# Moving a third of GpSimd's scaling, two sums and six masks to other places in a fused linear-attention and feed-forward kernel

## The chip, the core and the metric

The kernel runs on one core of a Trainium2 chip. The metric is device time in microseconds (us) of one execution. A core has five engines that each work off their own instructions in order and wait for each other through semaphores: TensorE (PE in the profile; its weight loads are the row PEld), VectorE (DVE), ScalarE (ACT), GpSimd (POOL) and SyncE (SP), which here only issues DMAs. TensorE writes to PSUM, which VectorE and ScalarE read; the kernel lets GpSimd work on SBUF alone.

## The reference

Two stages. The first is attention with a decaying state: for each of 4 batches and 8 heads, over blocks of a sequence of 768 with head size 64,

```python
intra = np.einsum('bhic,bhjc->bhij', qb, kb) * Dmask[None]      # lam ** (i - j), lower triangle
intra = np.einsum('bhij,bhjd->bhid', intra, vb)
inter = np.einsum('bhid,bhde->bhie', qb * lam_pow[None], kv_state)
out[:, :, sl] = intra + inter
kv_state = lam_block * kv_state + np.einsum('bhsd,bhse->bhde', kb * rev_pow, vb)
```

The second stage takes this output as x, 3072 tokens by 512, and computes `((x @ w_a) * (x @ w_b)) @ w_out` with 1536 inner features. Inputs and output are float32.

## The kernel before

**Units and groups.** A unit is 128 tokens of one batch with all its heads; there are 24, numbered 0 to 23, six to a batch. The feed-forward part takes them in seven groups of 4, 2, 4, 4, 4, 4 and 2 units (`GROUPS`, L28), numbered 0 to 6. While a group's feed-forward part runs on TensorE, the attention of the next group's units is worked in between, piece by piece.

**Pieces of a unit's attention.** "P" (`prep_k`, L301) scales k and then q by powers of lam into bfloat16, two GpSimd instructions (L276), lets SP issue a DMA transpose of the result (L310) and loads of q and k of a later unit (`pump`, L194), and lets GpSimd issue the load of v (L298). "S" (`piece_S`, L446) multiplies keys with queries, eight matmuls of 64 rows into two PSUM banks kq (L343), and lets VectorE mask both banks (`mask`, L360), the one right behind the other. "V", "O2" and "Q" bring the state forward and compute the unit's output; "Q" has the scores of one more unit in it. The last output piece of a group lets VectorE build four sums of x, `xs` (L542 to L545), that the next group's feed-forward part needs.

**The feed-forward part of groups 1 to 6** (`ffn_seven`, L550) computes 2-by-2 block products with seven multiplications in place of eight. Its *first step* forms the products with w_a and w_b in six blocks of features, i = 0 to 5 (the two-unit groups, whose tiles are cut otherwise, are not touched by the change). Each block has seven products m1 to m7 of four matmuls 128x256 (groups of four units). They run over steps s: block i does m1 at s = 7i, m5 at 7i+2, m2 at 7i+3, m6 at 7i+4, m3 at 7i+6, m7 at 7i+8 and m4 at 7i+12; the last m4 runs inside the second step. What the others do for a block:

- m1 into bank q; ScalarE copies it (s1). m5 into bank r; ScalarE copies it (s5). m6 is added into q; ScalarE copies that (u2). m3 is added into r; m7 and m4 are added into q.
- c11 = s1 + m2. Either VectorE adds it straight from PSUM (L598), or ScalarE copies m2 (s2, the rows `s<-m_p`) and GpSimd adds the two (L601). `SUM_ON_VEC` (L42) lists the blocks that go the first way.
- c12 = u2 + r on VectorE (L609, two buffers); GpSimd multiplies ab = c11 * c12 (L611).
- c22 = s5 + q on VectorE after m7 (L615); after m4 VectorE multiplies ab = c22 * q (L618). m4 is added into the bank that c22 reads, so it waits for c22.

The *second step* of groups 2 to 5 (`out_seven`, L657) multiplies ab with w_out in the same manner; its first product o_q reads the ab of blocks 0, 2 and 4.

**What sets the order.** Everything is written out by hand: each engine runs its instructions in the order of the program. `hook(slot)` calls, between the products, the pieces that `PLAN[g]` lists for that slot. In the first step, an even slot 2n comes behind step s = 7n+1 and an odd slot 2n+1 behind s = 7n+4: slot 1 behind s = 4, slot 2 behind 8, slot 4 behind 15, slot 5 behind 18, slot 6 behind 22, slot 7 behind 25, slot 8 behind 29. Slots 12 and more are in the second step; slots 17, 18 and 19 follow each other, with only the last product o_q<-two,ab and a store behind them. "G" at slot 17 is a GpSimd copy of one element of `xs` (L1008): GpSimd's later work waits for the sums. PSUM has seven banks for all this; `ps_bank` (L123) takes the one that was used longest ago among those that are not held.

In the kernel before, group 3 scales units 17, 18 and 19 in its first step and 20 at slot 17; group 4 scales 21, 22 and 23 in its first step. Units 15, 18+19 and 22+23 get their "S" at slot 7 of group 3, at slots 18 and 19 of group 3, and at slots 18 and 19 of group 4.

Of the kernel before, what the change touches and what calls it, by code (L numbers as in the profile page):

```python
# [17 lines left out]
BF16 = mybir.dt.bfloat16  # L18
# [4 lines left out]
def _bc(ap, dims):  # L23
    import dataclasses
    return dataclasses.replace(ap, ap=dims)
# [13 lines left out]


S_GROUPS = (1, 2, 3, 4, 5, 6)
SUM_ON_VEC = {1: (2,), 2: (0, 1, 2, 3, 5), 3: (1, 2, 3, 4, 5), 4: (1, 2, 3, 4, 5), 5: (1, 2, 4, 5), 6: (0, 1, 2)}  # L42
O_SEVEN = (2, 3, 4, 5)
O_EARLY = (5,)
ACT_COPY = (4, 10, 12, 13, 14, 16, 17, 18, 20, 21)
# [17 lines left out]
}  # L63
for _g, _u in ((2, 10), (3, 14), (4, 18)):
    PLAN[_g] += [(11, "V", _u), (13, "Q", (_u, _u + 1, _u + 2)), (14, "V", _u + 2), (14, "S", _u + 3),
                 (16, "O2", (_u + 2, _u + 3)), (18, "S", _u + 4)] + ([(19, "S", _u + 5)] if _g > 2 else [])
PLAN[2] += [(_s, "W", None) for _s in (3, 3, 3, 4, 4, 4)]


# [1 line left out]
def kernel(  # L71
# [11 lines left out]
    nc = tc.nc  # L83
    B, H, S, D = q.shape
    BLK = 128
    NB = S // BLK
    HP = H // 2
# [13 lines left out]
    msk_pool = ctx.enter_context(tc.tile_pool(name="msk", bufs=4))  # L101
# [11 lines left out]
    bank = {"held": set(), "age": [0] * 7, "clock": 0}  # L113

    def touch(i):
        bank["clock"] += 1
        bank["age"][i] = bank["clock"]
# [5 lines left out]
    def ps_bank(name, shape, dt, hold=False, at=None):  # L123
        i = at
        if i is None:
            i = min((i for i in range(7) if i not in bank["held"]), key=lambda i: bank["age"][i])
        touch(i)
        if hold:
            bank["held"].add(i)
        bank["last"] = i  # L130
        return ps_pool.tile(shape, dt, name=name, tag=f"ps{i}")

    def read(i):
        if i is not None:
            touch(i)
# [54 lines left out]
    def wait_for(t):  # L190
        landed = singles.tile([1, 1], t.dtype, name="landed")
        nc.sync.dma_start(out=landed, in_=t[0:1, 0, 0:1])
# [68 lines left out]
    lotri_bc = _bc(lotri, [lotri.ap[0], [0, HP], lotri.ap[1]])  # L261
# [7 lines left out]
    U = {}  # L269
# [17 lines left out]
    def make_ks(u, eng):  # L287
        scale(eng, qk_of(u)[:, 1], raw.pop((u, "k")), lp_k[:, u % NB])

    def make_qs(u, eng):  # L290
        scale(eng, qk_of(u)[:, 0], raw.pop((u, "q")), lp_q[:, u % NB])
# [3 lines left out]
    def make_vb(u):  # L295
        b, nb = divmod(u, NB)
        vb = prep_pool.tile([128, H, D], BF16, name="vb", tag="vb", bufs=7)
        nc.gpsimd.dma_start(out=vb, in_=vr[b, nb])  # L298
        vbs[u] = vb

    def prep_k(u):  # L301
        make_ks(u, "dve" if u < n0 + 4 else "pool")
        make_qs(u, "pool")
        scaled(u)

    def scaled(u):
        used["u"] = u + 1
        if u in DMA_T:
            qkT = qkT_pool.tile([128, 2, HP, 128], BF16, name="qkT", tag="qkT")
            nc.sync.dma_start_transpose(  # L310
                out=qkT[:].rearrange("p j hp i -> p (j hp) i"),
                in_=U[u]["qk"][:].rearrange("p j h d -> p (j h d)"))
            U[u]["qT"], U[u]["kT"] = qkT[:, 0], qkT[:, 1]
        pump()

    def piece_T(u):
        d = U[u]
        tps = ps_bank("tps", [128, 2, HP, 128], BF16)
        for j in range(2):
            for hp in range(HP):  # L320
                nc.tensor.transpose(tps[:, j, hp, :], d["qk"][:, j, 2 * hp:2 * hp + 2, :], ident)
        qkT = qkT_pool.tile([128, 2, HP, 128], BF16, name="qkT", tag="qkT")
        nc.scalar.copy(qkT, tps)
        d["qT"], d["kT"] = qkT[:, 0], qkT[:, 1]
# [4 lines left out]
    def score_banks():  # L329
        kq = Banks()  # L330
        kq.ids = []
        for i in range(2):
            kq.append(ps_bank(f"kq{i}", [128, HP, 128], F32))
            kq.ids.append(bank["last"])
        return kq

    def scores(u, kq=None):
        d = U[u]
        kq = kq or score_banks()
        for hp in range(HP):  # L340
            for i in range(2):
                p = slice(64 * i, 64 * i + 64)
                nc.tensor.matmul(kq[i][:, hp, :], lhsT=d["kT"][p, hp, :], rhs=d["qT"][p, hp, :],  # L343
                                 start=True, stop=True, skip_group_check=True)
        return kq

    def masks(u, kq):
        ms = mask(kq)
        U[u]["m"] = lambda i, hp: ms[i][:, hp, :]

    def mask(kq, split=False):
        ms = []
        for i in range(2):
            m = msk_pool.tile([128, HP, 128], BF16, name=f"m{i}", tag=f"m{i}")
            if split and i == 1:
                raw_kq = a_pool.tile([128, HP, 128], BF16, name="raw_kq", tag="a")
                nc.scalar.copy(raw_kq, kq[i])
                nc.gpsimd.tensor_mul(m, raw_kq, lotri_bc)
            else:
                nc.vector.tensor_mul(m, kq[i], lotri_bc)  # L360
            read(getattr(kq, "ids", (None, None))[i])
            ms.append(m)
        return ms
# [81 lines left out]

    def piece_S(u):  # L446
        masks(u, scores(u))

    def piece_V(u):
        kv_update(u)  # L450
        if u % NB < NB - 1:
            kv_copy(u, kv["ps"], "act" if u in ACT_COPY else "dve")
# [97 lines left out]
    def ffn_seven(g, u0, n, xT, hook, last):  # L550
# [31 lines left out]
        def step(i, n):  # L582
# [10 lines left out]
            elif n == 2:  # L593
                p, pb = bank_of("m_p")
                product(i, p, w_of(wa_sb, 2, i), x12, True)
                d["c11"] = a_pool.tile([128, nf, h], BF16, name="c11", tag="a")
                if i in SUM_ON_VEC[g]:
                    nc.vector.tensor_add(d["c11"], d["s12"][:, 0], p)  # L598
# [184 lines left out]
    def store_kept():  # L783
        row, o_sb = kept.pop(0)
        nc.sync.dma_start(out=out_r[row], in_=o_sb)
# [62 lines left out]
    def new_xT(g):  # L848
        gx[g] = xT_pool.tile([128, KS, 512], BF16, name="xT", tag="xT")
        for i in range(GROUPS[g]):  # L850
            xTs[g_u0[g] + i] = (gx[g], i * BLK)
# [62 lines left out]
    for u in range(n0):  # L914
        U[u] = dict(kn=kn4[:, u], qT=xT4["q"][:, :, u * BLK:(u + 1) * BLK],
                    m=lambda i, hp, u=u: ms4[hp // 2, u // 2][i][:, 2 * (u % 2) + hp % 2, :])
# [61 lines left out]
    for g, n in enumerate(GROUPS):  # L978
        if g + 1 < len(GROUPS):
            new_xT(g + 1)  # L980
        plan = {}
        for slot, name, us in PLAN.get(g, ()):
            plan.setdefault(slot, []).append((name, us))

        def hook(slot, plan=plan):
            for name, us in plan.get(slot, ()):
                if name == "P":
                    prep_k(us)
                    if us in DMA_T:
                        make_vb(us)  # L990
                elif name == "QS":
                    make_qs(us, "pool")
                elif name == "KS":
                    make_ks(us, "dve")
                    scaled(us)
                elif name == "LS":
                    wait_for(raw[us - 2, "k"])
                    load_x("q", us, nc.sync)
                    load_x("k", us, nc.sync)
                elif name == "L":  # L1000
                    load_all(us)
                elif name == "TW":
                    w_sums(us)
                elif name == "TO":
                    wo_sums(us)
                elif name == "G":
                    gate = singles.tile([1, 1], BF16, name="gate")
                    nc.gpsimd.tensor_copy(gate, xs[max(xs)][0:1, 3, 0, 0:1])  # L1008
                elif name == "GT":
                    gate = singles.tile([1, 1], BF16, name="gate")  # L1010
                    nc.gpsimd.tensor_copy(gate, two[max(two)][0:1, 3, 0, 0:1])
                elif name == "W":
                    store_kept()
                elif name == "T":
                    piece_T(us)
                elif name == "S":
                    piece_S(us)
                elif name == "V":
                    piece_V(us)
                elif name == "O":  # L1020
                    pieces_O((us,))
                elif name == "O2":
                    pieces_O(us)
                else:
                    pieces_O(us[:2], us[2:])

        if g in S_GROUPS:
            ffn_seven(g, g_u0[g], n, gx.pop(g), hook, g + 1 == len(GROUPS))
        else:
            ffn(g_u0[g], n, gx.pop(g), hook, g == 0)  # L1030
# [29 lines left out]
```

## Time and profile before

| | us |
|---|---|
| Median of 4 runs (218.99 to 219.17) | 219.06 |
| The profiled execution, its own time | 218.99 |
| Its span, first to last instruction | 216.9 |
| PE, PEld, DVE busy in the span | 209.6, 162.7, 175.3 |
| ACT, POOL busy in the span | 109.1, 126.6 |
| First matmul of the first step of groups 2, 3, 4, 5 | 72.63, 105.03, 138.09, 169.94 |

TensorE is busy for 97% of the span, at a granted clock of 0.998. Busy does not mean at its best: a matmul's row has the time that it spends in the pipeline (273 ns for 128x256), while in a steady stream one starts every 109 ns, a product of four every 0.437 us. Losses are therefore read from the distance between the starts of two products, and from the chain of waits.

### The profile page before, as it was taken

The page shows a single profiled execution, that of the slowest core. Times are in us where ns is not written, and L with a number is a line of the kernel's source. Part 1 is how long each engine was busy: PE and PEld are TensorE (multiplying, and loading weights), DVE is VectorE, ACT ScalarE, POOL GpSimd, SP SyncE. Part 2 cuts the span into 40 slices and gives each one's busy share as a digit, 9 for nine tenths or more (in the row PEclk, how much of TensorE's full clock was granted, in tenths as well). Part 3 has the DMA queues.
Part 4 walks back from the last instruction along what each step waited for, and adds up shares of the span by engine and source line. Part 5 has one row for each costly group of instructions (what it writes and reads, how often), then busy time and mean ns, then how long its engine had stood idle before and what let it go on. Part 6 is the DMA issues. An engine that isn't in the chain of part 4 may idle for free.

```text
span 216.9 us, 5801 instructions
## 1 busy us (share of the span) xinstructions
PE 209.6 (97%) x2339; PEld 162.7 (75%) x2347; DVE 175.3 (81%) x320; ACT 109.1 (50%) x199; POOL 126.6 (58%) x144
## 2 busy tenths in 40 slices
PE   7799999999999999999999999999999999999993
PEld 2376444555996788878888887888987888889973
DVE  0892999878788987999588999788999787996860
ACT  2686224256872556436555535465535557343521
POOL 5879659973697199810999920699810246400320
PEclk9999999999999999999999999999999999999999
DMA  4999999999799989992699994499900500002202
GB/s 125 302 180 193 202 231 213 229 219 176 122 196 158 158 96 265 156 276 40 130 201 251 175 217 75 128 233 115 111 3 3 193 3 0 3 0 90 108 3 97
DMA packets 84654, 30.78 MB, mean 142 GB/s; under 512 B 71956, under 2 KB 81044, under 8 KB 84628
## 3 DMA queue, kind: packets, MB, share of 16 engines
q1 hardware_dynamic: 51636, 19.86, 45.7%
q0 software_dynamic: 32704, 10.49, 42.2%
q8 instruction: 18, 0.29, 0.6%
q10 hardware_dynamic: 288, 0.07, 0.1%
q14 instruction: 8, 0.07, 0.1%
HBM read 28.32 MB, written 6.29 MB: 160 GB/s over the span
## 4 chain that ended last, share of the span: by engine, by line
PE 84%; POOL 7%; DMA 3%; SPq 1%; ACT 1%; DVE 1%; issue 1%
PE m_q L564 20%; PE m_r L564 10%; PE op L801 10%; PE o_q L675 9%; PE o_r L675 5%; PE o_ps L379 5%; PE m_p L564 5%; PE b_ps L487 5%; PE a_ps L487 5%; PE kq L343 3%; POOL qk L276 3%; DMA k<-in_k_dram 3%; POOL ab L611 3%; PE o_p L675 2%; PE kvd L410 1%; SPq L229 1%
## 5 line engine op out<-in xcount | busy, mean ns | idle before, releaser
L564 PEld LDWEIGHTS <-tw 128*128 128x128 bf16 x576 | 48.9, 98 | 5.8 <-issue 0.3
L611 POOL TENSOR_TENSOR ab<-c,c 128x512 bf16<-128x512 bf16 x30 | 34.8, 1168 | 28.5 <-DVE c L609 28.2
L564 PE MATMUL m_q<-xs,tw 128*128 128x256 bf16 (+1 forms) x288 | 36.1, 255 | 0.0
L360 DVE TENSOR_TENSOR m<-kq,lotri 128x512 bf16<-128x512 f32 x47 | 29.5, 682 | 1.5 <-PE kq L343 1.5
L564 PEld LDWEIGHTS <-wa_sb 128*128 128x128 bf16 x288 | 24.7, 98 | 2.6
L579 ACT COPY s<-m_q 128x512 f32<-128x512 f32 x30 | 17.7, 590 | 17.1 <-PE m_q L564 15.5
L618 DVE TENSOR_TENSOR ab<-c,m_q 128x512 bf16<-128x512 f32 x30 | 20.6, 686 | 6.7 <-PE m_q L564 4.5
L609 DVE TENSOR_TENSOR c<-u,m_r 128x512 f32<-128x512 f32 x30 | 20.5, 682 | 5.9 <-ACT u L579 5.3
L298 POOL DMA_DIRECT2D vb<-in_v_dram x24 | 22.4, 933 | 1.5 <-DMA wo_sb<-in_moe_w_out_dram 1.2
L801 PE MATMUL op<-wo_sb,ab 128*128 128x512 bf16 (+2 forms) x114 | 22.1, 335 | 0.4 <-issue 0.2
L579 ACT COPY s<-m_r 128x512 f32<-128x512 f32 x30 | 17.7, 590 | 7.2 <-PE m_r L564 7.2
L579 ACT COPY u<-m_q 128x512 f32<-128x512 f32 x30 | 17.8, 595 | 6.3 <-PE m_q L564 6.0
L615 DVE TENSOR_TENSOR c<-s,m_q 128x512 f32<-128x512 f32 x30 | 20.6, 685 | 0.5
L675 PEld LDWEIGHTS <-sm 128*128 128x128 bf16 x192 | 17.5, 98 | 3.6 <-DVE sm L714 0.4
L598 DVE TENSOR_TENSOR c<-s,m_p 128x512 bf16<-128x512 f32 x23 | 15.8, 687 | 4.7 <-PE m_p L564 4.5
L276 POOL TENSOR_TENSOR qk<-qf,lp_q 128x512 bf16<-128x512 f32 x18 | 18.8, 1044 | 1.2 <-DMA qf<-in_q_dram 1.2
L601 POOL TENSOR_TENSOR c<-s 128x512 bf16<-128x512 f32 x7 | 9.1, 1293 | 16.4 <-ACT s L579 16.4
L402 ACT CAST xT<-o_ps 128x512 bf16<-128x512 f32 x22 | 11.9, 589 | 12.7 <-PE o_ps L379 12.4
L564 PE MATMUL m_q<-xT,tw 128*128 128x256 bf16 (+1 forms) x144 | 18.1, 255 | 0.1
L564 PE MATMUL m_r<-xs,tw 128*128 128x256 bf16 (+1 forms) x144 | 18.1, 255 | 0.0
L564 PE MATMUL m_q<-xT,wa_sb 128*128 128x256 bf16 (+1 forms) x144 | 18.1, 255 | 0.0
L564 PE MATMUL m_r<-xs,wb_sb 128*128 128x256 bf16 (+1 forms) x144 | 18.1, 255 | 0.0
(119 smaller groups left out, 375.6 us busy)
## 6 DMA issues: line engine op xcount, KB each, us to landing
out_dram<-o_two SPq DMA_DIRECT2D x8, 512.0 KB, 3.6
qf<-in_q_dram SPq DMA_DIRECT2D x14, 256.0 KB, 5.0
kf<-in_k_dram SPq DMA_DIRECT2D x14, 256.0 KB, 5.6
vb<-in_v_dram POOLq DMA_DIRECT2D x24, 128.0 KB, 5.5
wa_sb<-in_moe_w_a_dram POOLq DMA_DIRECT2D x6, 256.0 KB, 6.2
wb_sb<-in_moe_w_b_dram POOLq DMA_DIRECT2D x6, 256.0 KB, 7.6
wo_sb<-in_moe_w_out_dram POOLq DMA_DIRECT2D x6, 256.0 KB, 8.1
out_dram<-o_kept SPq DMA_DIRECT2D x6, 256.0 KB, 4.5
```

Of the source, the lines that this page charges most:

```text
L276: eng_of(eng).tensor_mul(dst.rearrange("p (c b) d -> p b c d", b=2), x[:].rearrange("p (b c) d -> p b c d", b=2), lp.rearrange("p (b c) o ...
L298: nc.gpsimd.dma_start(out=vb, in_=vr[b, nb])
L360: nc.vector.tensor_mul(m, kq[i], lotri_bc)
L487: nc.tensor.matmul(ps[:, lo:hi], lhsT=w_sb[:, s, f * 128:(f + 1) * 128], rhs=xT[:, s, lo:hi], start=(s == 0), stop=(s == KS - 1), skip_gro ...
L564: nc.tensor.matmul(ps[:, f, :], lhsT=w(k, f), rhs=x[:, k, :], start=(first and f == 0 and k == 0), stop=True, skip_group_check=True)
L579: nc.scalar.copy(t, ps)
L609: nc.vector.tensor_add(c12, d["u2"], d["r"])
L611: nc.gpsimd.tensor_mul(ab[:, nf * i:nf * i + nf, 0:h], d["c11"], c12)
L615: nc.vector.tensor_add(d["c22"], d["s5"], d["q"])
L618: nc.vector.tensor_mul(ab[:, nf * i:nf * i + nf, h:2 * h], d["c22"], d["q"])
L675: nc.tensor.matmul(ps[:, t, :], lhsT=x(j, c)[:, t * BLK:(t + 1) * BLK], rhs=w(j)[:, c, :], start=(first and t == 0 and j == js[0] and c == ...
L801: nc.tensor.matmul(op[:, lo:hi], lhsT=ab[:, f, t * 128:(t + 1) * 128], rhs=wo_sb[:, f, lo:hi], start=(f == 0), stop=(f == FC - 1))
```

## The change

Three things change, in groups 3, 4 and 5 alone. The order of all instructions up to 105 us in the profile stays.

- **Scaling.** Units 17 and 18, and 21 and 22, stay in the first step (slots 2 and 5 in place of 1 and 4). Units 19 and 23 move from slot 7 of the first step to slot 17, behind the gate on the sums of x, unit 19 ahead of unit 20.
- **Sums.** In groups 3 and 4 the c11 of block 0 is added by VectorE too; ScalarE's copy s2 and GpSimd's add of that block go.
- **Masks.** Unit 15 gets its scores at slot 6 of group 3 in place of slot 7; units 19 and 23 move from slot 19 of groups 3 and 4 to slot 6 of groups 4 and 5. The scores and the mask of the first bank come at slot 6, the mask of the second bank at slot 8; that bank is held in between.

```diff
-SUM_ON_VEC = {..., 3: (1, 2, 3, 4, 5), 4: (1, 2, 3, 4, 5), 5: (1, 2, 4, 5), 6: (0, 1, 2)}
+SUM_ON_VEC = {..., 3: range(6), 4: range(6), 5: (1, 2, 4, 5), 6: (0, 1, 2)}
...
-    3: [(1, "P", 17), (4, "P", 18), (7, "S", 15), (7, "P", 19), (17, "G", None), (17, "P", 20)],
-    4: [(1, "P", 21), (4, "P", 22), (7, "P", 23)],
-    5: [(11, "V", 22), (13, "O2", (22, 23))],
+    3: [(2, "P", 17), (5, "P", 18), (6, "SA", 15), (8, "SB", 15), (17, "G", None), (17, "P", 19), (17, "P", 20)],
+    4: [(2, "P", 21), (5, "P", 22), (6, "SA", 19), (8, "SB", 19), (17, "G", None), (17, "P", 23)],
+    5: [(6, "SA", 23), (8, "SB", 23), (11, "V", 22), (13, "O2", (22, 23))],
...
-                 (16, "O2", (_u + 2, _u + 3)), (18, "S", _u + 4)] + ([(19, "S", _u + 5)] if _g > 2 else [])
+                 (16, "O2", (_u + 2, _u + 3)), (18, "S", _u + 4)]
...
+    def piece_SA(u):
+        kq = U[u]["kq"] = scores(u)
+        U[u]["ms"] = [mask_one(kq, 0)]
+        return [kq.ids[1]]
+
+    def piece_SB(u):
+        ms = U[u]["ms"]
+        kq = U[u].pop("kq")
+        ms.append(mask_one(kq, 1))
+        U[u]["m"] = lambda i, hp: ms[i][:, hp, :]
+        return [kq.ids[1]]
+
+    def mask_one(kq, i):
+        m = msk_pool.tile([128, HP, 128], BF16, name=f"m{i}", tag=f"m{i}")
+        nc.vector.tensor_mul(m, kq[i], lotri_bc)
+        read(kq.ids[i])
+        return m
...
+                elif name == "SA":
+                    bank["held"].update(piece_SA(us))
+                elif name == "SB":
+                    bank["held"].difference_update(piece_SB(us))
```

More of the change, by code (lines that the diff above doesn't have):

```diff
@@ L41 @@
 S_GROUPS = (1, 2, 3, 4, 5, 6)
-SUM_ON_VEC = {1: (2,), 2: (0, 1, 2, 3, 5), 3: (1, 2, 3, 4, 5), 4: (1, 2, 3, 4, 5), 5: (1, 2, 4, 5), 6: (0, 1, 2)}
+SUM_ON_VEC = {1: (2,), 2: (0, 1, 2, 3, 5), 3: range(6), 4: range(6), 5: (1, 2, 4, 5), 6: (0, 1, 2)}
 O_SEVEN = (2, 3, 4, 5)
```

## The prediction

> **What bounds the kernel now.** First the busy line of the page: TensorE is the engine to watch, and whatever does not delay it costs nothing.
>
> ```profile
> PE 209.6 (97%) x2339; PEld 162.7 (75%) x2347; DVE 175.3 (81%) x320; ACT 109.1 (50%) x199; POOL 126.6 (58%) x144
> PE 84%; POOL 7%; DMA 3%; SPq 1%; ACT 1%; DVE 1%; issue 1%
> ```
>
> The second line, the chain that ended last, has GpSimd for 7%, and the chain in order of time, asked for 104 to 126 us, shows where: in group 3, in one piece (start, length, engine and line).
>
> ```profile
> 108.50 0.67 DVE c L615
> 109.16 0.02 issue
> 109.18 1.29 POOL c L601
> 110.47 2.00 POOL qk L276 x2
> 112.46 0.88 POOL vb L298
> 113.34 0.02 issue
> 113.36 2.30 POOL ab L611 x2
> 115.66 1.99 POOL qk L276 x2
> 117.65 0.89 POOL vb L298
> 118.54 0.02 issue
> 118.56 1.18 POOL ab L611
> 119.74 2.00 POOL qk L276 x2
> 121.73 0.88 POOL vb L298
> 122.61 0.02 issue
> 122.63 2.31 POOL ab L611 x2
> 124.94 0.05 issue
> 124.98 1.05 PE o_q L675 x8
> ```
>
> GpSimd has no gap; the second step's o_q ends up waiting for its product ab of block 4. Last, the timeline of TensorE for 114 to 126 us: the two places where a product starts late.
>
> ```profile
> 118.74 0.60 PE L564 MATMUL m_q<-xs,tw 128*128 128x256 bf16 x4
> 119.49 0.60 PE L564 MATMUL m_q<-xT,tw 128*128 128x256 bf16 x4
> ...
> 124.98 1.05 PE L675 MATMUL o_q<-wo_sb,ab 128*128 128x256 bf16 x8 [0.31 <-POOL ab L611]
> ```
>
> The columns are start, length, engine and line, operation, tiles and shapes, and in brackets idle time with what ended it. A product starts 0.437 us after the one before; here m4 starts 0.749 after it. GpSimd is only part of it: group 4, without such places, is shorter than group 3 by 33.06 - 31.85 = 1.21 us, of which 0.44 is unit 15's scores. So everything that can be gained in group 3 is 0.8 us, however long GpSimd's chain looks.
>
> **The change, part by part.** Every term is a delay of TensorE, read from product starts in the profiled execution.
>
> *1. o_q's wait, group 3: -0.48.* o_q takes 1.788 us in group 3 and 1.310 in group 4. GpSimd loses the add (1.29) and unit 19 (119.69 to 122.61, 2.9). Worked forward: unit 16 done at 109.16, ab 0 (1.17 each) at 110.3, unit 17 (3.0) at 113.3, ab 1 at 114.5, unit 18 at 117.5, ab 2 at 118.7, ab 3 at 119.9, ab 4 once its c12 is there, at some 122.8. o_q wants it at 124.5 and no longer waits; 1.7 us are to spare.
>
> *2. m4's wait, group 3: -0.31.* c22 came late, at 118.76: VectorE had waited 0.61 us at 114.57 for a c12 buffer (ab 0 freed it at 114.5; now at 110.3), and then did both masks of unit 15 in one go, 116.37 to 117.65. 0.749 - 0.437 = 0.31.
>
> *3. The copy s2, groups 3 and 4: -0.11 each.* m7 of block 0 starts 0.547 us after the product before it (107.28, 107.83), since u2 is copied behind s2 (106.67). Group 2, where block 0 is summed on VectorE already, has 0.436. VectorE is free then: it waits 2.34 us ahead of 107.81.
>
> *4. Unit 19's and 23's scores leave the end of groups 3 and 4: -0.14 each.* From the start of the last scores to the next group it takes 1.874 us with sixteen of their matmuls (136.22 to 138.10), 1.872 in group 4, and 1.734 with eight in group 2. Why so little: with eight, o_q<-two,ab waits for the add L769, which the other eight had hidden; that is in the 1.734.
>
> *5. They come back inside groups 4 and 5: +0.43 each.* Unit 15's eight matmuls stretch two steps of 0.437 to 1.310 us: 0.44. Eight more in a row cost only 0.554 - 0.330 = 0.22 (the scores' rows at 136.22 and 115.78); the other half goes at the two changes between 128-row and 64-row matmuls. In groups 3 and 4 a pair of changes was shared by two units. Unit 15 itself only moves.
>
> *6. VectorE's load: 0.* It gets one more sum per group (0.69) in groups 3 and 4. Group 4 has it busy for 15.1 of 18.3 us; with the sum and two masks of 0.62 (four back to back took 2.48) it is 17.0 of 18.6. Step by step: the mask of slot 6 runs while the scores hold TensorE anyway. The mask of slot 8 sits ahead of c11, which was ready 0.94 us after c22's start and now starts at 1.24; the four operations of a block take 2.5 of 3.06 us, so the delay is down to 0.04 at the next c22, which has 0.6 of slack ahead of m4. If that cover is gone, the price is 0.31 per place, as in term 2.
>
> *7. Other waits: 0.* Unit 19 scaled behind the gate: in group 3, unit 15's transpose was issued 0.3 us after the group's start; the DMA view of 103 to 120 us has 7.0 us to landing, and slot 6 comes 9.6 us after the start: 2 to spare. Unit 22's loads queue on SP behind that transpose; unit 18's did in group 3, were issued by 107.7, took 6.3 and would be wanted at 114.5 (group start plus 9.5), so 0.5 remains, and a late one uses up term 1's spare before it costs. The store of group 3's second half waits on SP behind two transposes; nobody waits for it. Unit 23's scaling (3 us) meets a GpSimd that idles 14.31 us before 172.33. The held bank: at most six of seven are in use by my count; the trace has no row for holding one, so between 0 and the 0.31 of a late product in each of three groups; I take 0, as TensorE's rows show no wait for a bank in the first steps. It cannot gain.
>
> *A rule that speaks against it.* VectorE's adds take 0.69 us both in group 3, with GpSimd busy 18.97 of 19.05 us, and in group 5, with 8.37 of 18.26; but the two sums L708, which read SBUF twice, took 0.75 at 93.67 and 1.62 at 125.04 beside GpSimd's ab. The Trainium skill (Perfetto Trace Analysis, Optimizing Scalar/DVE Operations) says that moving work between these two might not help, since they share a port to SBUF. Taken so, the c11 that moves would double and the gain of term 3 might go, -0.21 in place of -0.43 in all; but c11 reads one operand from PSUM, as the 0.69 rows do.
>
> *Sum.* -0.48 - 0.31 - 0.22 - 0.28 + 0.86 = -0.43: 218.99 becomes 218.56, and the median 219.06, which lies 0.07 above the profiled execution, 218.63. I predict **218.6 us**, 0.2% less.
>
> **Rivals.**
>
> *GpSimd stays late (no change).* Group 4 now begins with two units behind the gate, as group 3 did, and unit 22's load may come late; then o_q waits as before, in either group: 0.48 comes back, 219.05 us. For it: the chain of group 3 was full from 103 us on. Against: 4.2 us of work leave it. It decides once GpSimd is over 1.7 us later than worked out.
>
> *VectorE turns late (slower).* One place, slot 8: the mask ahead of c11 pushes the next c22 past m4's start. Price 0.31 in each of groups 3, 4 and 5, 0.94 in all: 219.5 us. For it: at 91% in the first step there is little room, and term 2 was such a case. Against: the 0.61 wait that began term 2 is gone, and a single mask is half as long. It decides once c22 starts over 0.6 us late.
>
> **How the numbers follow.** The forecast, with 0.1 either way and up to 0.3 for small gains in the waits beside it, 218.3 to 218.75: 0.70; GpSimd late, near 219.05: 0.15; VectorE late, 219.5: 0.15. A measurement of this kernel tells some 0.2%, 0.44 us, from no change. My forecast stands on that edge (218.62): I split its 0.70 into 0.50 faster and 0.20 within. So faster 0.50, within 0.35, slower 0.15. The range 218.3 to 219.15 takes in the first two cases.
>
> **What would show it.** Right: no GpSimd piece in the chain between 105 and 125 us; m4 behind each c22 at 0.437; m7 of block 0 at 0.437 in groups 3 and 4; group lengths 32.0 (group 3), 32.0 (group 4) and group 5 longer by 0.43; 19's and 23's scores with a step of 0.53 ahead of them. Wrong: o_q released by POOL ab, a late m4 after slot 8 of any group, or scores that wait for a transpose; or scores that cost other than 0.43 in their new place.

## The result, and the profile after

| | before | after |
|---|---|---|
| Median, us | 219.09 (218.81 to 220.88, 53 runs) | 218.56 (218.28 to 220.03, 32 runs) |
| The profiled execution, its own time and span, us | 218.99, 216.9 | 220.39, 218.7 |
| A second profiled execution of after, unchanged ("again") | | 218.51, 216.8 |

The ratio after to before is 0.9979, 95% interval 0.9971 to 0.9987: 0.53 us by the medians. 218.6 was forecast. The measured 0.21% sits on the 0.2% that the forecast called the edge of no change, and the interval (0.13% to 0.29%) reaches to both sides of it.

The total came out within 0.07 us, but not by its own terms: below, one term of it fails by 0.23 us, and most of the gain lies where the prediction had not looked. That the total agrees is luck, though six of its seven terms hold.

The first profiled execution of after is 1.88 us longer than that of "again". 0.52 of that lies ahead of group 1 and 1.35 in it, in instructions that the change leaves alone; groups 3, 4 and 5 agree within 0.007 us. Rows are therefore shown from "again", and only the page's busy line and the shares of the chain that ended last from the first profile of after:

```profile
PE 210.7 (96%) x2339; PEld 163.0 (75%) x2347; DVE 177.3 (81%) x322; ACT 108.7 (50%) x197; POOL 124.7 (57%) x143
PE 90%; DMA 3%; DVE 2%; SPq 1%; ACT 1%; issue 1%; DVEq 0%
```

GpSimd, 7% of the chain before, is no longer in the list, though its busy time fell by 1.9 us only. The chain in order of time shows the same for 104 to 126 us in "again" (start, length, engine and line):

```profile
103.79 1.47 PE o_q L693 x12
105.26 0.44 PE m_q L582 x4
...
113.62 0.87 PE m_q L582 x8
114.50 0.33 PE kq L343 x8
114.83 0.54 PE m_r L582 x4
...
123.23 0.44 PE m_q L582 x4
123.67 0.22 PE kvd L410 x4
123.89 1.31 PE o_q L693 x12
```

Where GpSimd stood from 109.2 to 124.9 us, TensorE stands from end to end. GpSimd's own timeline in "again" (start, length; in brackets idle time ahead and what ended it) says why:

```profile
108.28 0.94 POOL L298 DMA_DIRECT2D vb<-in_v_dram  x1
109.23 1.17 POOL L629 TENSOR_TENSOR ab<-c,c 128x512 bf16<-128x512 bf16 x1
...
116.42 0.94 POOL L298 DMA_DIRECT2D vb<-in_v_dram  x1
117.37 2.29 POOL L629 TENSOR_TENSOR ab<-c,c 128x512 bf16<-128x512 bf16 x2
121.19 1.16 POOL L629 TENSOR_TENSOR ab<-c,c 128x512 bf16<-128x512 bf16 x1 [1.52 <-DVE c L627]
```

The first ab ends at 110.40, worked out were 110.3. The two ab ahead of block 4's end at 119.66, worked out was 119.9. From there GpSimd waits 1.52 us for VectorE, not TensorE for GpSimd.

TensorE's timeline in "again", the places of m4 and o_q:

```profile
118.70 0.60 PE L582 MATMUL m_q<-xs,tw 128*128 128x256 bf16 x4
119.14 0.60 PE L582 MATMUL m_q<-xT,tw 128*128 128x256 bf16 x4
...
123.73 1.47 PE L693 MATMUL o_q<-wo_sb,ab 128*128 128x256 bf16 x12
125.04 1.04 PE L693 MATMUL o_p<-wo_sb,ab 128*128 128x256 bf16 x8
```

m_q<-xT,tw is m4: 0.44 behind the product before it (0.749 before). o_q takes 125.04 - 123.73 = 1.31 (1.788 before), without brackets.

**Where the time went**, by the distance from the first matmul of a group's first step to that of the next (us; groups 2 and 6 agree within 0.01):

| | group 3 | group 4 | group 5 | sum |
|---|---|---|---|---|
| before | 33.060 | 31.841 | 28.927 | |
| again (after) | 32.037 | 32.267 | 29.362 | |
| difference | -1.023 | +0.426 | +0.435 | -0.16 |
| forecast | -1.04 | +0.18 | +0.43 | -0.43 |

The last row adds the prediction's terms by group. The three differences make 0.16 us of the 0.53. Most of the rest is not in the recorded span: own time less span is 1.98 to 2.11 us in 29 executions of before (median 2.04) and 1.65 to 1.74 in 12 of "again" (1.70), 0.34 us apart by the medians, and the two ranges don't meet. The median span of those executions is 216.9 us in before and 216.85 in "again".

### The profile page after: what moved, and what is told of

Same layout as the page of the kernel before. It is cut to its first block, busy times and chain, and to the rows that moved or that the text cites. A ratio compares the mean times of both kernels' runs of the same rounds, so it can differ in the third digit from the quotient of the medians.

```text
span 218.7 us, 5797 instructions
## 1 busy us (share of the span) xinstructions
PE 210.7 (96%) x2339; PEld 163.0 (75%) x2347; DVE 177.3 (81%) x322; ACT 108.7 (50%) x197; POOL 124.7 (57%) x143
## 4 chain that ended last, share of the span: by engine, by line
PE 90%; DMA 3%; DVE 2%; SPq 1%; ACT 1%; issue 1%; DVEq 0%
PE m_q L582 23%; PE m_r L582 12%; PE op L819 10%; PE o_q L693 9%; PE m_p L582 6%; PE o_r L693 5%; PE o_ps L379 5%; PE b_ps L505 5%; PE a_ps L505 5%; PE kq L343 3%; DMA k<-in_k_dram 3%; PE o_p L693 2%; PE kvd L410 1%; SPq L229 1%; PE tps L321 1%
## 5 line engine op out<-in xcount | busy, mean ns | idle before, releaser
L360 DVE TENSOR_TENSOR m<-kq,lotri 128x512 bf16<-128x512 f32 x41 | 25.9, 682 | 0.9 <-PE kq L343 0.9
L616 DVE TENSOR_TENSOR c<-s,m_p 128x512 bf16<-128x512 f32 x25 | 17.1, 686 | 6.7 <-PE m_p L582 5.8
L582 PE MATMUL m_p<-xT,wa_sb 128*128 128x256 bf16 (+1 forms) x144 | 18.1, 255 | 0.7 <-DVE m L360 0.7
```

The source lines that it names most:

```text
L582: nc.tensor.matmul(ps[:, f, :], lhsT=w(k, f), rhs=x[:, k, :], start=(first and f == 0 and k == 0), stop=True, skip_group_check=True)
```

## The experiments

All times are medians; "ratio" is to the kernel before on the same chip, with its 95% interval. "Groups" are the lengths of groups 3, 4 and 5 in that run's profile. The line numbers of after are 18 above those of before in the feed-forward part.

**again** is after, unchanged: is the long group 1 of after's first profile part of it?

> The kernel after, unchanged, for a second profile. The first one has 1.8 us more than the median: 0.53 us before the first transpose and 1.36 us in group 1 (m5 of block 1 and a transpose behind it), where VectorE's scaling of a k took 1.79 us beside a GpSimd add in place of 0.69; both lie in parts that the change leaves alone. Theory (a chance meeting in that execution): 218.5 to 218.6 us and a profile without the 1.36; then the groups last 32.40 (2), 32.04 (3), 32.03 (4), 29.36 (5). Rival (the change moved something that makes VectorE meet GpSimd in group 1): the 1.79 row is there again.

218.56 us, 218.37 to 219.49, ratio 0.9981 (0.9970 to 0.9992). Its profiled execution took 218.51, and group 1 was 19.459 us as in before, not 20.811. Group 4 took 32.267 in place of the expected 32.03; old_sums and the runs behind it show why. The excess belongs to that execution alone; what it was most likely is told at the end.

**before_again** is before, unchanged: was the profile from which the terms were read a lucky one?

> The kernel before, unchanged, for a second profile and as the measure of what the comparison itself can tell. The first profile of before spans 216.9 us in an execution of 218.99, 2.1 us around it; the kernels after and its variants have 1.7 around theirs. Theory (the same instructions, the same time): within 0.1% of the other runs of before, group lengths 32.40, 33.06, 31.84, 28.93, the waits of 0.31 and 0.48 in group 3 again. Rival (the first profile was a lucky one for its groups): the groups come out longer, which would mend why the medians differ by more (0.4 to 0.5) than the group lengths of the two profiles (0.16).

219.01 us, ratio 1.0008 (0.9991 to 1.0025). Groups 33.030, 31.850, 28.927, m4 0.725, o_q 1.780; outside the span 2.06. The terms were read from a typical execution. The rival of a lucky profile falls, and the 0.34 us outside the span stays to be explained.

**pairs** takes the masks' splitting away, from after: both masks at slot 6, none at slot 8.

> The kernel after, but units 15, 19 and 23 get both masks in one go at slot 6; slot 8 is empty and no bank is held. Theory (it is the place, not the splitting: at slot 6 the masks run behind c22 and the scores give VectorE 0.43 us more; worked forward, the next c22 is done 0.15 us before m4 wants it): no change against the kernel after, within 0.1 us, and no late m4. Rival (two masks in one go make c22 late wherever they are): m4 waits 0.2 to 0.3 in each of groups 3, 4 and 5, 0.6 to 0.9 more, 219.2 to 219.5 us.

```diff
-    3: [..., (6, "SA", 15), (8, "SB", 15), ...],
+    3: [..., (6, "S", 15), ...],
(the same for 19 in group 4 and 23 in group 5)
```

218.60 us, ratio 0.9986 (0.9969 to 1.0003). Groups 32.036, 32.260, 29.361: those of after, with no late m4. At slot 6 a pair delays TensorE no more than two single masks do; that the place counts is shown by sums_slot6_shift below.

**old_sums** takes the sums away, from after: GpSimd adds block 0 again.

> The kernel after, but block 0's c11 in groups 3 and 4 is copied by ScalarE and added by GpSimd again. Theory (moving a unit out of the first step frees GpSimd by itself; the sums only save m7's delay): m7 of block 0 starts 0.547 behind the product before it in groups 3 and 4, o_q does not wait: +0.22 against the kernel after, 218.78 us. Rival (GpSimd needs the add taken away too): besides the 0.22, a c12 waits for its buffer or o_q for ab in groups 3 and 4, +0.3 to +0.5 each: 219.3 us or more.

```diff
-SUM_ON_VEC = {..., 3: range(6), 4: range(6), ...}
+SUM_ON_VEC = {..., 3: (1, 2, 3, 4, 5), 4: (1, 2, 3, 4, 5), ...}
```

218.60 us, ratio 0.9978 (0.9962 to 0.9994). Groups 32.137, 32.143, 29.361. o_q doesn't wait: with one unit less to scale, GpSimd is in time with the add too. m7 is back at 0.547 in both groups, as expected; group 3 pays its 0.10, but group 4 is shorter than in after, by 0.12. There m6 to m3 is 0.490 again, and it was 0.719 in "again". So the sums save 0.11 in group 4 and something that comes with them costs 0.23. Only ScalarE's s5 stands between these two products: m3 is added into the bank r that s5 reads. ScalarE's timeline in "again":

```profile
137.34 0.58 ACT L795 COPY o_two<-o_q 128x512 f32<-128x512 f32 x1 [3.83 <-PE o_q L693]
137.82 0.59 ACT L597 COPY s<-m_q 128x512 f32<-128x512 f32 x1
138.54 0.58 ACT L597 COPY s<-m_r 128x512 f32<-128x512 f32 x1
```

s5 starts 0.72 behind s1, and no releaser stands beside it; m5, on which it waits, had released it at 138.19, some 0.35 ahead of s5's start (138.54), and in old_sums s5 starts 0.07 to 0.09 behind the matching moment. s5 is here the 192nd ScalarE instruction that the trace records if the waits that it lists are counted, and the 128th without them. In old_sums s1 has both numbers, and s1 has to wait for o_two anyway.

**sums_only** makes the sums alone, in before.

> The kernel before with the one edit that VectorE adds block 0's c11 in groups 3 and 4; three units are still scaled in group 3's first step and the masks stay where they were. Theory (GpSimd was late by less than the 1.29 us of its add, and the copy s2 held up m7): m7's 0.11 goes in both groups, o_q's wait of 0.48 goes (worked forward, block 4's ab is done at 123.8, wanted at 124.1), and m4's wait shrinks from 0.31 to some 0.18, since unit 15's two masks in one go make c22 late by themselves: -0.83, 218.25 us, faster than the kernel after. Rival (two units in place of three are needed to free GpSimd): o_q still waits some 0.4 and m4 0.31; -0.22 to -0.3, 218.8 us.

```diff
-SUM_ON_VEC = {..., 3: (1, 2, 3, 4, 5), 4: (1, 2, 3, 4, 5), ...}
+SUM_ON_VEC = {..., 3: range(6), 4: range(6), ...}
```

218.07 us (217.93 to 218.36), ratio 0.9958 (0.9944 to 0.9973). That is lower than after: no execution of it took as long as the shortest of "again" (218.37), which ran beside it. The expected 218.25 had neither the late s5 nor the shorter time outside the span in it. Groups 32.339, 31.973, 28.927. No o_q wait and no late m7, with all three units still scaled in the first step; m4 is still late, 0.604 (0.749 before), because both masks of unit 15 sit at slot 7. In group 4 m6 to m3 is 0.720, s5 having the same number as in after.

**sums_shift** asks whether that late s5 hangs on its place in ScalarE's stream: sums_only and one more ScalarE instruction, a copy of one element, ahead of it.

> The kernel before with block 0's c11 on VectorE in groups 3 and 4 (the run sums_only), and one more ScalarE instruction, a copy of one element, at slot 17 of group 3, where ScalarE is idle for 3 us. All runs that leave out the copies s2 of groups 3 and 4 showed the copy s5 of block 0 in group 4 0.25 us late (m6 to m3 0.72 us in place of 0.49), though what it waits for was there. Theory (a gap in ScalarE's supply of instructions at a fixed place of its stream, the 192nd of its recorded instructions, that the removed copies moved under s5): with one instruction more the place falls on another one with slack, m6 to m3 in group 4 is 0.49, 0.23 less than sums_only, some 217.85 us. Rival (s5 waits for the copy s1 ahead of it, which is there whenever s2 does not follow): 0.72 stays, and the time is sums_only's 218.07 or a little more.

```diff
-    3: [..., (17, "G", None), ...],
+    3: [..., (17, "A", None), (17, "G", None), ...],
...
+                elif name == "A":
+                    mark = singles.tile([1, 1], F32, name="mark")
+                    nc.scalar.copy(mark, lam_sb[0:1, 0:1])
```

Groups 32.335, 31.738, 28.925: m6 to m3 in group 4 is 0.491, and the group 0.235 shorter by one instruction more. The total is less clear, 218.30 us, ratio 0.9956 (0.9938 to 0.9974), against 218.07 without the copy. One reason is the time up to group 1, which no edit touches and which scatters: that group's first matmul comes between 52.98 and 53.83 us in the profiles of this study.

**after_shift** is the same test on after itself.

> The kernel after with one more ScalarE instruction, a copy of one element, issued at slot 17 of group 3. Theory (a gap in ScalarE's supply of instructions at a fixed place of its stream is what made group 4 longer than forecast): s5 of block 0 comes on time in group 4, its m6 to m3 is back at 0.49 and the group at 32.03 us in place of 32.267, the forecast's 32.0; group 3 stays at 32.04, group 5 at 29.36; the time 218.3 if the time outside the span stays at 1.7. Rival (the late s5 belongs to the schedule of after, not to the place in the stream): group 4 stays at 32.27.

Its edit is that of sums_shift, made to after. Groups 32.028, 32.030, 29.361: group 4 is the 32.0 of the forecast. ScalarE's timeline in after_shift, where s5 follows s1 by 0.47:

```profile
138.40 0.59 ACT L597 COPY s<-m_q 128x512 f32<-128x512 f32 x1
138.87 0.60 ACT L597 COPY s<-m_r 128x512 f32<-128x512 f32 x1
```

And m6 and m3 on TensorE in after_shift, 0.49 apart, and then in "again", 0.72 apart:

```profile
139.04 0.60 PE L582 MATMUL m_q<-xs,tw 128*128 128x256 bf16 x4
139.53 0.60 PE L582 MATMUL m_r<-xs,wb_sb 128*128 128x256 bf16 x4
```

```profile
138.46 0.60 PE L582 MATMUL m_q<-xs,tw 128*128 128x256 bf16 x4
139.18 0.60 PE L582 MATMUL m_r<-xs,wb_sb 128*128 128x256 bf16 x4
```

The rival, that the late s5 belongs to the schedule of after, falls. The gain is more than one profile's: the shortest span of 12 executions is 216.2 us, and 216.7 in "again". The time is 218.54 us, ratio 0.9975 (0.9961 to 0.9990), not the 218.3 expected: 0.14 of the 0.24 is given back in the time outside the span, which is now 1.84.

**before_shift** puts the same copy into before, where no product can gain by it: does the time outside the span move?

> The kernel before with the same one-element copy on ScalarE at slot 17 of group 3, nothing else. Theory on the span: no product moves, groups 33.04, 31.85, 28.93 and a span of 216.9. On the time outside the span, which was 2.06 us in before and 1.7 in every kernel with the sums on VectorE: if it depends on how ScalarE's instructions fall, it may change here with nothing else changed, to 1.7 and 218.7 us; if it hangs on the copies s2 or on GpSimd's adds that left, it stays at 2.06 and the time at 219.05.

Its edit is that of sums_shift, made to before. Groups 33.051, 31.850, 28.926, as before. Outside the span: 2.24 us (2.02 to 2.34 in 12 executions, 2.05 in before beside it); 219.20 us, ratio 1.0007 (0.9992 to 1.0022). Neither of the two expected values: it moved, upward. So this time can change while the groups don't; it moved by 0.19 with one instruction that nothing waits for. Why was not found.

**sums_slot6_shift** leaves out what seems to cost: sums_shift, and unit 15's scores with both masks at slot 6.

> The run sums_shift, and unit 15's scores and both masks at slot 6 of group 3 in place of slot 7. Theory (at slot 6 both masks fit behind c22, as the run pairs showed; GpSimd with three units and no add is early enough by 0.3 us): m4's wait of 0.17 goes, o_q does not wait, 0.17 less than sums_shift, some 217.7 us, and the fastest of all. Rival (with three units in the first step GpSimd has no slack and slot 6 takes it): o_q or a c12 waits for GpSimd, 0.1 to 0.4 of it lost again.

```diff
-    3: [..., (7, "S", 15), (7, "P", 19), ...],
+    3: [..., (6, "S", 15), (7, "P", 19), ...],
```

217.73 us (217.40 to 218.38), ratio 0.9938 (0.9918 to 0.9957). Groups 32.174, 31.732, 28.925. m4 of the place that was late, in sums_shift (0.60 behind the product before it) and then in sums_slot6_shift (0.43):

```profile
119.29 0.60 PE L564 MATMUL m_q<-xs,tw 128*128 128x256 bf16 x4
119.89 0.60 PE L564 MATMUL m_q<-xT,tw 128*128 128x256 bf16 x4
```

```profile
118.82 0.60 PE L564 MATMUL m_q<-xs,tw 128*128 128x256 bf16 x4
119.25 0.60 PE L564 MATMUL m_q<-xT,tw 128*128 128x256 bf16 x4
```

Every wait that the change removes is gone here without moving unit 19's and 23's scaling or scores.

**scores_inside** prices the scores' move by itself: the sums and unit 15 at slot 6, and units 19 and 23 at slot 6 of groups 4 and 5; the scaling stays as in before. (It has no copy at slot 17.)

> The price of terms 4 and 5 alone: all sums on VectorE in groups 3 and 4, unit 15 at slot 6, three units scaled in the first step as in before; but the scores and masks of units 19 and 23 go from the end of groups 3 and 4 to slot 6 of groups 4 and 5 (both masks in one go). Theory (a pair of changes between 128-row and 64-row matmuls is no longer shared): two times 0.43 - 0.14 = 0.58 more than the same kernel with the scores at the end, which by sums_only less its m4 wait is 217.9: some 218.45 us. Rival (the scores cost only their own streaming, since they were worked before too): 217.9 us.

```diff
-    3: [..., (7, "S", 15), ...],
-    4: [(1, "P", 21), (4, "P", 22), (7, "P", 23)],
-    5: [(11, "V", 22), ...],
+    3: [..., (6, "S", 15), ...],
+    4: [(1, "P", 21), (4, "P", 22), (6, "S", 19), (7, "P", 23)],
+    5: [(6, "S", 23), (11, "V", 22), ...],
...
-                 (16, "O2", ...), (18, "S", _u + 4)] + ([(19, "S", _u + 5)] if _g > 2 else [])
+                 (16, "O2", ...), (18, "S", _u + 4)]
```

218.70 us, ratio 0.9996 (0.9979 to 1.0013); the expected 218.45 left out the late s5, which is here too (m6 to m3 0.719). Groups 32.033, 32.258, 29.361. Against sums_slot6_shift, group 3 gains 0.141, group 5 loses 0.436, and group 4, less the 0.235 of the late s5, loses 0.29 (0.436 in, 0.14 out): 0.59 us in all for a move that brings nothing. And the groups are those of after to 0.01: with the sums made, moving the scaling adds nothing either.

**sum5** goes one step on from sums_slot6_shift: c11 of block 0 on VectorE in group 5 too.

> The best kernel so far (before with the sums of groups 3 and 4 on VectorE, unit 15's scores at slot 6, the one-element copy on ScalarE at slot 17 of group 3), and c11 of block 0 on VectorE in group 5 as well. Theory (m7 of block 0 is late where ScalarE copies s2 ahead of u2): m7 falls from 0.545 to 0.437 us in group 5, the group from 28.925 to 28.82, the time from 217.73 to 217.6. Rival (ScalarE's stream is one instruction shorter from here on, and its gap falls on another copy; or VectorE runs late without the GpSimd sum): another product of group 5 or 6 is late by 0.1 to 0.25 and the gain is gone, 217.7 to 217.9.

```diff
-SUM_ON_VEC = {..., 5: (1, 2, 4, 5), ...}
+SUM_ON_VEC = {..., 5: (0, 1, 2, 4, 5), ...}
```

217.50 us (217.32 to 218.13), ratio 0.9930 (0.9912 to 0.9948); group 5 is 28.819, 0.106 shorter, as the theory has it. TensorE's rows of m1 of block 1 and m7 of block 0 in group 5, in "again" (0.55 apart) and then in sum5 (0.44):

```profile
171.65 0.60 PE L582 MATMUL m_q<-xT,wa_sb 128*128 128x256 bf16 x4
172.20 0.60 PE L582 MATMUL m_q<-xs,tw 128*128 128x256 bf16 x4
```

```profile
171.01 0.60 PE L564 MATMUL m_q<-xT,wa_sb 128*128 128x256 bf16 x4
171.45 0.60 PE L564 MATMUL m_q<-xs,tw 128*128 128x256 bf16 x4
```

It has the lowest median of this study, 1.47 us below before in the same runs, and its bounds and those of after don't touch (0.9912 to 0.9948; 0.9971 to 0.9987). From sums_slot6_shift it is told apart by group 5 alone, not by the times.

## Why the prediction was right, and where it was wrong

**Term 1, o_q's wait, -0.48: right in size.** 1.788 to 1.310. But the wait needed only one of the two reliefs: the sums alone end it (sums_only), and so does the scaling's move, with the masks' beside it, without the sums (old_sums). The prediction worked GpSimd's time out with both and did not ask which was needed.

**Term 2, m4, -0.31: right.** 0.749 to 0.437 in "again". sums_only splits it: an earlier GpSimd alone brings 0.145, the place of the masks the other 0.167 (0.604 to 0.437). The split of the masks brings nothing (pairs).

**Term 3, the copy s2, -0.11 each: the step that failed, in group 4.** m7 comes on time in both groups, so the copy's price was right. The prediction took it that a copy less can only help. In group 4 of after, s5 came 0.25 us later than m5 allows and held up m3: +0.23 beside the -0.11. That the late s5 costs the group this much, and that it comes from which instructions stand ahead of it on ScalarE, is shown by after_shift: with one instruction more, s5 is on time and group 4 is 32.030, the forecast 32.0. Why s5 is late was not found; what fits is told at the end. No row of before showed such a delay, so the term could not have had it, but it gave no bound for one either.

**Terms 4 and 5, the scores' move, -0.14 each and +0.43 each: right.** Group 5 is longer by 0.435, group 4 loses 0.29 and group 3 gains 0.14 by scores_inside. Unit 23's scores in group 5 of "again", with 0.53 and 0.33 for two starts where one would take 0.437:

```profile
178.31 0.60 PE L582 MATMUL m_q<-xs,tw 128*128 128x256 bf16 x4
178.84 0.40 PE L343 MATMUL kq<-qkT 64*128 64x128 bf16 x8
179.17 0.61 PE L582 MATMUL m_r<-xs,tw 128*128 128x256 bf16 x4
179.62 0.60 PE L582 MATMUL m_p<-xT,wa_sb 128*128 128x256 bf16 x4
```

From kq's predecessor to the next product but one it takes 1.31 in place of 0.874. The Trainium skill (TensorEngine Tiling (Array Packing), Key Properties) says that changing the tiling mode drains TensorE, without a price. The steps of 0.53 into and 0.45 out of the 64-row matmuls, where a step is 0.437, fit a drain of some 0.1 us at the entry; the trace shows the delay, not what makes it.

**Terms 6 and 7, VectorE and the other waits, 0: right.** From block 1 on TensorE's steps in "again" are 0.437, block after block, behind slot 8 too; the scores at slot 6 start 0.53 behind the product before them, which is the price of the change of tile, so no transpose was late; no bank was waited for. The doubt that the sums would double in length beside GpSimd did not come true: the sum that moved, block 0's in group 3, takes 0.69 at 106.68 in "again", while GpSimd scales a unit beside it.

**The rivals.** GpSimd did not stay late, with 1.5 us of waiting ahead of block 4's ab; VectorE did not turn late.

**Outside the terms.** Groups 3, 4 and 5 together fell by 0.16 us where 0.43 was forecast. That the total agrees is due to the 0.34 us outside the span, which the prediction had as a constant. The same quantity is 1.67 in sums_only, 1.73 in old_sums, 1.84 in after_shift, 1.88 in sums_slot6_shift, 2.24 in before_shift, and 1.71 to 1.73 in the other four edited kernels (medians). What sets it stays open: neither the copies nor the adds that leave order these values. Without it, after would be 0.16 to 0.2 us below before, about half the width of the interval of the ratio (0.35 us from end to end).

In sum, of the four things in the change the sums carry the gain, unit 15's slot helps, the scaling's move is a second remedy for a wait that the first has ended, and moving units 19's and 23's scores costs 0.59 us, which the prediction had priced at 0.58.

## What to carry to other kernels

When a change has several parts that relieve the same wait, work out each part alone: the second remedy brings nothing, and here a part that came with it had a price. Move short bursts of another matmul shape together, not apart. And when a total agrees, check it by its terms and by the span: a sum can be right by two errors, here a gain in the groups that was forecast 0.27 us too large, and 0.34 us outside the span that was not forecast.

## What the runs showed of the hardware

**A ScalarE instruction can start late with nothing to wait for, and one instruction more ahead of it ends that.** s5 of block 0 starts 0.25 us late in group 4 of after, pairs, sums_only and scores_inside, and on time in sums_shift and after_shift, where one more instruction stands ahead of it. That the delay hangs on the instructions ahead is shown. That it sits at a fixed number is not: counted without waits, the late s5 is the 128th and in after_shift s1 is, where a gap would be hidden behind o_two; counted with them, the 192nd is in after_shift a wait between s1 and s5, and it comes 0.39 behind s1 as in "again", not later.

That the loading of instructions is behind it is a guess, but the traces have a sign of it. They record loads of instructions as DMA packets of their own kind. In "again" one of 8 KB on queue q14 starts at 141.48, 2.94 us behind the late s5. In after_shift it starts at 137.43, 0.97 ahead of s1, though the edit adds one ScalarE instruction and nothing else. In all five profiles with a late s5 that load comes 2.8 to 3.1 us behind it; in the eight others it comes 0.8 to 1.1 ahead of s1. Delay and load move together; that the one makes the other is not shown.

**The time outside the recorded span differs from build to build.** Its medians go from 1.67 to 2.24 us, while the executions of each build but before_shift (0.32) lie within 0.2 us of each other.

**A VectorE instruction that reads SBUF twice meets GpSimd in group 1.** The 1.35 us in group 1 of after's first profile begin with VectorE's scaling of k. Its timeline there, and then GpSimd's:

```profile
56.29 1.79 DVE L276 TENSOR_TENSOR qk<-qkf,lp_k 128x512 bf16<-128x512 f32 x1 [0.89 <-DMA qkf<-in_k_dram]
58.00 0.68 DVE L443 TENSOR_TENSOR st<-kvd,bdiag 128x512 bf16<-128x512 f32 x1
```

```profile
56.27 1.26 POOL L619 TENSOR_TENSOR c<-s 128x512 bf16<-128x512 f32 x1
```

In "again" the same scaling takes 0.69:

```profile
55.29 0.69 DVE L276 TENSOR_TENSOR qk<-qkf,lp_k 128x512 bf16<-128x512 f32 x1 [0.86 <-DMA qkf<-in_k_dram]
```

k landed half a microsecond later against the group's start (2.54 us behind it, 2.06 in "again"), just behind GpSimd's add, and the scaling took 1.10 us longer; the masks behind it came late and held an m_p up by 0.91 us, and an m4 behind that came 0.46 late. The Trainium skill (SBUF — State Buffer, Who interferes with whom) says that a VectorE instruction with two SBUF inputs contends with a GpSimd instruction that reads SBUF, that the shared ports are an exclusive lock, and that the order of issue decides who blocks. The rows agree: the scaling ends at 58.08, 0.55 us behind the end of GpSimd's add, which is most of an undisturbed scaling. In scores_inside the scaling starts first, 0.14 us ahead of the add, and takes 0.71, while the add takes 1.70. The same products are late there, with k 1.36 us late, so a load that is late enough does it without a longer scaling.
